# A state-space scan with hash routing: the spreading of states, the first routing steps and the first parity masks change engine and place

## The chip, the cores and the metric

The kernel runs on one core of a Trainium2 chip. A core has five engines, each with a queue of its own that it works off in order: TensorE (PE in the profile; PEld are its weight loads), VectorE (DVE), ScalarE (ACT), GpSimd (POOL) and SyncE (SP), which here only issues DMAs. They wait for one another through semaphores. The metric is the time of one execution on the device in microseconds; lower is better.

## The reference

A Mamba-2 scan (4 batches, 8 heads, 768 positions, head width 32, 16 states) writes a tensor of 3072 tokens by 256, and a mixture of 8 experts runs on it, each token going to the expert that a hash of its id names:

```python
log_a = np.log(np.clip(a, 1e-06, 1.0))
for c in range(nc):                       # chunks of 32 positions
    cum = np.cumsum(log_a[chunk])
    M = (Cc @ Bc.T) * np.exp(cum_i - cum_j) * causal
    y[chunk] = M @ xc + (Cc @ state) * np.exp(cum)
    state = np.exp(sum(log_a[chunk])) * state + (Bc * np.exp(cum_last - cum)).T @ xc
x = y.transpose(0, 2, 1, 3).reshape(3072, 256)
expert = token_ids * 2654435761 % 8
for e in range(8):
    out[expert == e] = np.maximum(x[expert == e] @ w1[e], 0) @ w2[e]
```

## The kernel before

The program has three parts: a prologue (decays, first batch's transposes), the scan over 24 output chunks of 128 positions (six a batch), and the expert layers, which gather the stored tokens by indirect DMA and scatter the results the same way. In the first two parts the order on each engine is the order in which the code is written.

The work is in steps of 64 positions, 12 to a batch. For a batch `b` the code names its steps so:

- `rows(b, i)`: scales B (i = 0) or C (i = 1) by decay factors; VectorE for batch 0, GpSimd for the others. `put_steps` and `get_steps` send the scaled B through memory (`b_steps`) and back as `bs`, in another layout; for batch 0 `turn_steps` does this on TensorE.
- `turn_b`, `turn_c`: eight transposes each on TensorE into PSUM (`tp`, two buffers), evicted by ScalarE to `bt`, `ct` and the two parity masks `ce` (C with the heads of one parity kept). `cp` is C times the step's decay, on GpSimd.
- `states(b, half)`: small products on TensorE (24 or 20), then on VectorE the recurrence `st` over six or five steps, each reading the product in PSUM.
- `blocks`: spreads each state over a block matrix `up`, with zeros for the other heads, by a product with a 0/1 pattern `own`.
- `grams(gc)`: the products of B and C for chunk `gc` (`gram`, two PSUM buffers), then on VectorE `m`, the causal mask times them.
- `outputs(gc)`: y in PSUM (`y_ps`, one buffer) from `cp` and `up` (line 487), and from x and `m` (line 496); ScalarE copies it to `y_sb`, SyncE stores it to `y_tokens`.

The loop over `gc` does `grams(gc + 1)`, `outputs(gc)`, the next piece of `routing()`, then, by the chunk's place in its batch, one of the steps of the next batch and a load. `routing()` is a generator that finds, from the token ids, where each token goes: `eid`, `mask`, counts by two matmuls (220, 221) into a `gram` buffer, a scan `pre`, the number of overflow tiles `nov`, `jump`, `val`, `slot`, `past`, four products `at`, three products `of`, 24 index matmuls (299) and `tokens`. Each `yield` ends a piece. The weights of the first three experts are loaded from ScalarE's queue from chunk 7 on.

`spin` issues matmuls whose result nobody reads; they are fillers on TensorE. In the prologue there are 10 on `ones`, 6 on `cum` and 2 more on `ones`.

## Time and profile before

| | us |
|---|---|
| median of 3 runs | 329.01 (327.29 to 330.5) |
| the profiled execution | 330.96, its span 329.2 |
| TensorE busy | 283.1 (86% of the span), 2507 matmul records |
| VectorE, GpSimd, ScalarE busy | 105.7, 102.9, 54.0 |
| mean granted TensorE clock | 0.885 |
| last y matmul of the scan | about 102.4 |
| first matmul of the expert layers | 117.30 |

The profile gives times from the start of the span. [...] Idle time of an engine is put down to what ended it (the releaser). A row of the timeline may merge neighbours of one kind: x20 is twenty of them, and a float32 matmul has two records. The expert layers run at the full clock with TensorE nearly always busy; the prologue and the scan, a third of the time, are where engines wait.

### The profile page before, as it was taken

Reading aid. Unit: us, or ns where it says so; the run is one execution under the profiler, and the core shown is the slowest. Engines: PE = TensorE matmul, PEld = TensorE weight load, DVE = VectorE, ACT = ScalarE, POOL = GpSimd, SP = SyncE. Lnnn points to the kernel's source line nnn. Section 1 sums busy time; section 2 is a strip of 40 time slices with the busy share of each in tenths; the row PEclk is TensorE's granted clock in tenths of the full one; section 3 lists DMA queues with packets and bytes.
Section 4 is the critical chain, followed back from the end, with each engine's and each line's share of the span. In section 5 each row is a group of like instructions: output and inputs, shape, how many; then the busy total and the mean of one; then the engine's idle time right before and its main releaser. Section 6 shows DMA issues by size and latency. Waiting matters only on the chain.

```text
span 329.2 us, 6084 instructions
## 1 busy us (share of the span) xinstructions
PE 283.1 (86%) x2507; PEld 178.5 (54%) x2507; DVE 105.7 (32%) x215; ACT 54.0 (16%) x116; POOL 102.9 (31%) x115
## 2 busy tenths in 40 slices
PE   7925986979983189999999999999999999999930
PEld 7724875858863045555555555555555555555510
DVE  3484489796541111211311211211211311211110
ACT  4300232415111001011111111111111111111110
POOL 6343045461210571311611612612611202202240
PEclk9997576585779559999999999999999999999985
DMA  7995379597479120144233243243342000000110
GB/s 124 157 132 147 77 142 195 143 223 196 137 244 324 52 81 28 32 148 142 73 144 138 82 151 126 84 156 114 90 169 96 31 2 16 31 0 19 34 48 2
DMA packets 56384, 35.65 MB, mean 108 GB/s; under 512 B 34911, under 2 KB 52345, under 8 KB 56356
## 3 DMA queue, kind: packets, MB, share of 16 engines
q1 hardware_dynamic: 49508, 22.41, 29.9%
q0 software_dynamic: 2816, 6.56, 6.3%
q10 hardware_dynamic: 4032, 6.29, 5.8%
q8 instruction: 20, 0.33, 0.4%
q14 instruction: 8, 0.07, 0.1%
HBM read 27.78 MB, written 7.73 MB: 108 GB/s over the span
## 4 chain that ended last, share of the span: by engine, by line
PE 53%; issue 19%; DVE 11%; DMA 10%; POOL 4%; ACT 1%; POOLq 0%; ACTq 0%; DVEq 0%
PE h_ps L613 18%; PE o_ps L622 16%; DMA out_dram<-o_sb,idx_out 6%; PE gram L470 4%; PE y_ps L496 4%; DVE st L449 3%; PE tp L404 3%; POOL out_dram L583 3%; PE y_ps L487 2%; DMA y_tokens<-y_sb 2%; PE y_ps L165 2%; PE tp L442 2%; PE xt_ps L601 1%; DVE m L474 1%; DVE at L286 1%
## 5 line engine op out<-in xcount | busy, mean ns | idle before, releaser
L613 PE MATMUL h_ps<-xT,w 128*128 128x416 f32 x256 | 102.7, 526 | 0.3 <-DVE xT L602 0.3
L622 PE MATMUL o_ps<-hT,w 128*128 128x416 f32 x256 | 102.1, 518 | 0.0
L622 PEld LDWEIGHTS o_ps<-hT,w 128*128 128x128 f32 x256 | 47.5, 190 | 40.1 <-issue 36.3
L583 POOL DMA_INDIRECT out_dram<-o_sb,idx_out x32 | 31.2, 976 | 114.0 <-ACT o_sb L642 95.8
L613 PEld LDWEIGHTS h_ps<-xT,w 128*128 128x128 f32 x256 | 47.5, 196 | 32.8 <-issue 31.1
L578 POOL DMA_INDIRECT xg<-y_tokens,idx_in x32 | 32.0, 1001 | 50.8 <-issue 20.1
L608 DVE TENSOR_SCALAR hT<-h_ps 128x416 f32<-128x416 f32 x32 | 18.9, 592 | 75.3 <-PE h_ps L613 75.3
L602 DVE COPY xT<-xt_ps 128x256 f32<-128x256 f32 (+1 forms) x32 | 12.0, 375 | 76.6 <-PE xt_ps L601 76.6
L606 ACT ACTIVATE hT<-h_ps 128x416 f32<-128x416 f32 x32 | 16.5, 517 | 99.8 <-PE h_ps L613 96.0
L496 PE MATMUL y_ps<-x_t,m 64*64 64x32 f32 x768 | 20.5, 250 | 7.3 <-DVE m L474 7.3
L496 PEld LDWEIGHTS y_ps<-x_t,m 64*64 64x64 f32 x768 | 20.0, 175 | 8.8 <-DVE m L474 8.7
L601 PE MATMUL xt_ps<-ident,xg 128*128 128x128 f32 (+1 forms) x64 | 12.6, 280 | 12.0 <-DMA xg<-y_tokens,idx_in 11.3
L474 DVE TENSOR_TENSOR m<-gram,causal 128x512 f32<-128x512 f32 x24 | 16.4, 687 | 17.9 <-PE gram L470 17.9
L601 PEld LDWEIGHTS xt_ps<-ident,xg 128*128 128x128 f32 (+1 forms) x64 | 8.4, 147 | 25.1 <-issue 23.0
L470 PE MATMUL gram<-ce,bt 32*64 32x128 f32 x384 | 21.1, 349 | 0.1
L457 POOL TENSOR_TENSOR up<-st,own 128x640 f32<-128x640 f32 (+1 forms) x8 | 13.1, 1640 | 24.2 <-DVE st L449 21.8
L500 ACT ACTIVATE y_sb<-y_ps 128x256 f32<-128x256 f32 x24 | 9.2, 383 | 63.1 <-PE y_ps L496 63.1
L642 ACT ACTIVATE o_sb<-ot_ps 128x256 f32<-128x256 f32 x16 | 6.1, 383 | 60.2 <-PE ot_ps L639 60.2
L470 PEld LDWEIGHTS gram<-ce,bt 32*64 32x64 f32 x384 | 13.6, 168 | 3.2 <-issue 2.1
L426 POOL TENSOR_TENSOR cp<-ct,step 128x768 f32<-128x768 f32 x4 | 6.1, 1529 | 26.1 <-ACT ct L417 26.1
L487 PE MATMUL y_ps<-up,cp 64*64 64x128 f32 x176 | 13.5, 359 | 0.6 <-ACT y_sb L500 0.6
L639 PE MATMUL ot_ps<-ident,oT 128*128 128x128 f32 (+1 forms) x64 | 12.2, 275 | 1.2 <-ACT oT L631 0.6
(123 smaller groups left out, 188.8 us busy)
## 6 DMA issues: line engine op xcount, KB each, us to landing
w<-in_moe_w_dram SPq DMA_DIRECT2D x20, 512.0 KB, 4.5
w<-in_moe_w_dram ACTq DMA_DIRECT2D x12, 512.0 KB, 5.4
y_tokens<-y_sb SPq DMA_DIRECT2D x24, 128.0 KB, 3.7
bc<-in_B_dram SPq DMA_DIRECT2D x4, 384.0 KB, 6.5
bc<-in_C_dram SPq DMA_DIRECT2D x4, 384.0 KB
x_t<-in_x_dram SPq DMA_DIRECT2D x4, 384.0 KB, 8.5
x_t<-in_x_dram SPq DMA_DIRECT2D x16, 96.0 KB, 3.3
b_steps<-rows SPq DMA_DIRECT2D x3, 384.0 KB, 4.0
```

The costliest lines, as they stand in the source:

```text
L457: eng.tensor_tensor(out=ups[b][:, k0:k1], in0=sts[b][:, k0:k1].unsqueeze(2).to_broadcast(sh), in1=own.rearrange("p g e d -> p g (e d)").un ...
L470: nc.tensor.matmul(out=gram[q * HL:(q + 1) * HL, g, u * P:(u + 1) * P], lhsT=bts[b][rr, 2 * c + u], rhs=ces[b][rr, :, 2 * c + u], start=Tr ...
L474: nc.vector.tensor_tensor(out=m.rearrange("p g u e i -> p g (u e i)"), in0=gram[:, :, 0:2 * P], in1=causal.rearrange("p (g x) i -> p g (x ...
L487: nc.tensor.matmul(out=y_ps[u * HL:(u + 1) * HL, q, 0:P], lhsT=cps[b][w, k], rhs=ups[b][w, k].rearrange("p g x -> p (g x)"), start=True, s ...
L496: nc.tensor.matmul(out=y_ps[u * HL:(u + 1) * HL, q, h * D:(h + 1) * D], lhsT=m[w, g, u, e], rhs=xs[b][w, h, k], start=(k == 0 and h == 0), ...
L578: nc.gpsimd.indirect_dma_start(out=dst, out_offset=None, in_=y_dram[:], in_offset=bass.IndirectOffsetOnAxis(ap=idx, axis=0), bounds_check= ...
L583: st = nc.gpsimd.indirect_dma_start(out=out[:], out_offset=bass.IndirectOffsetOnAxis(ap=idx, axis=0), in_=src, in_offset=None, bounds_chec ...
L601: nc.tensor.transpose(out=tp[:, i, 0:r], in_=g[0:r, i * P:(i + 1) * P], identity=ident[0:r, 0:r])
L606: nc.scalar.activation(o, i, AF.Relu)
L608: nc.vector.tensor_scalar_max(out=o, in0=i, scalar1=0.0)
L613: nc.tensor.matmul(out=hp, lhsT=w1s[e][:, i, f * P:(f + 1) * P], rhs=xT[e][:, i], start=(i == 0), stop=(i == DP - 1))
L622: nc.tensor.matmul(out=oP[e][:, j, 0:CAP], lhsT=w2s[e][:, f, j * P:(j + 1) * P], rhs=h, start=(f == 0), stop=(f == FP - 1))
```

## The change

- `blocks` no longer runs on GpSimd. The first piece of batch 0 stays on VectorE; every other call becomes four ScalarE instructions, one for each pair of pattern column and parity, with the 0/1 value as the scale. The calls stand later: one chunk behind the `states` whose result they spread.
- `routing()` is started at the top of the scan; its first piece stands before `turn_c(0)`, its second behind it, its third before the second `turn_steps`. So every later piece falls two chunks earlier than before.
- The second and third product `of` move from VectorE to GpSimd.
- The prologue has 3 fillers on `cum` instead of 6, and the 2 on `ones` are gone.
- The parity masks of batch 0 are four ScalarE instructions, two small ones (the first two steps) first; before, ScalarE did one parity and VectorE the other, in halves.

The diff:

```diff
--- before.py
+++ after.py
@@ -290,9 +290,9 @@
         nc.vector.tensor_tensor(out=of[:, 2], in0=iota_c.unsqueeze(1).to_broadcast(shc),
                                 in1=scol.unsqueeze(2).to_broadcast(shc), op=OP.is_equal)
         yield
-        nc.vector.tensor_tensor(out=of[:, 0], in0=of[:, 2], in1=iota_b.unsqueeze(2).to_broadcast(shc), op=OP.mult)
-        yield
-        nc.vector.tensor_tensor(out=of[:, 1], in0=of[:, 2], in1=one_ub.unsqueeze(2).to_broadcast(shc), op=OP.mult)
+        nc.gpsimd.tensor_tensor(out=of[:, 0], in0=of[:, 2], in1=iota_b.unsqueeze(2).to_broadcast(shc), op=OP.mult)
+        yield
+        nc.gpsimd.tensor_tensor(out=of[:, 1], in0=of[:, 2], in1=one_ub.unsqueeze(2).to_broadcast(shc), op=OP.mult)
         yield
         inv_ps = ps_t.tile([P, 512], F32, name="tp")[:, 0:2 * NM].rearrange("p (i x) -> p i x", i=2)
         for c in range(NCH):
@@ -318,7 +318,7 @@
     fac = apre.tile([NR, 2, BH, RS], F32)
     nc.scalar.activation(fac[:, 0], rel, AF.Exp, scale=-1.0)
     nc.scalar.activation(fac[:, 1], rel, AF.Exp)
-    spin(flat(cum), 6)
+    spin(flat(cum), 3)
 
     totx = apre.tile([NR, BH, NS], F32)
     step = const.tile([P, NB, NU], F32)
@@ -418,10 +418,9 @@
             if not first:
                 for e in range(2):
                     nc.scalar.activation(ce[:, e, :, rs], v, AF.Identity, scale=par[:, e:e + 1])
-        for p in range(0, NR, NR // 2) if first else ():
-            ps = slice(p, p + NR // 2)
-            nc.scalar.activation(ce[:, 0, ps], ct[:, ps], AF.Identity, scale=par[:, 0:1])
-            nc.vector.tensor_scalar(out=ce[:, 1, ps], in0=ct[:, ps], scalar1=par[:, 1:2], scalar2=None, op0=OP.mult)
+        for ps in (slice(0, 2 * RU), slice(2 * RU, NR)) if first else ():
+            for e in range(2):
+                nc.scalar.activation(ce[:, e, ps], ct[:, ps], AF.Identity, scale=par[:, e:e + 1])
         cp = abat.tile([P, NU, HL], F32, name="cp")
         nc.gpsimd.tensor_tensor(out=cp, in0=ct.rearrange("p (k c) r -> p k (c r)", c=RU),
                           in1=step[:, b].unsqueeze(2).to_broadcast([P, NU, HL]), op=OP.mult)
@@ -449,13 +448,19 @@
                 nc.vector.scalar_tensor_tensor(out=st[:, k + 1], in0=st[:, k], scalar=step[:, b, k:k + 1],
                                                in1=tp[:, i * PW:(i + 1) * PW], op0=OP.mult, op1=OP.add)
 
-    def blocks(b, k0, k1, eng):
+    def blocks(b, k0, k1, first=False):
 
         if b not in ups:
             ups[b] = abat.tile([P, NU, 2, PW], F32, name="up")
-        sh = [P, k1 - k0, 2, PW]
-        eng.tensor_tensor(out=ups[b][:, k0:k1], in0=sts[b][:, k0:k1].unsqueeze(2).to_broadcast(sh),
-                                in1=own.rearrange("p g e d -> p g (e d)").unsqueeze(1).to_broadcast(sh), op=OP.mult)
+        if first:
+            sh = [P, k1 - k0, 2, PW]
+            nc.vector.tensor_tensor(out=ups[b][:, k0:k1], in0=sts[b][:, k0:k1].unsqueeze(2).to_broadcast(sh),
+                                    in1=own.rearrange("p g e d -> p g (e d)").unsqueeze(1).to_broadcast(sh), op=OP.mult)
+            return
+        for g in range(2):
+            for e in range(2):
+                ds = slice(e * D, (e + 1) * D)
+                nc.scalar.activation(ups[b][:, k0:k1, g, ds], sts[b][:, k0:k1, ds], AF.Identity, scale=hm[:, g, e:e + 1])
 
     ms = {}
 
@@ -500,22 +505,23 @@
         nc.scalar.activation(y_sb, y_ps[:, :, 0:P], AF.Copy)
         nc.sync.dma_start(out=y_dram[gc * P:(gc + 1) * P, :], in_=y_sb.rearrange("p q d -> p (q d)"))
 
+    todo = iter(routing())
     rows(0, 0, nc.vector)
     turn_b(0)
     rows(0, 1, nc.vector)
     steps()
     heads()
-    spin(ones, 2)
+    next(todo)
     turn_c(0, True)
+    next(todo)
     turn_steps(0, 0)
     grams(0)
     states(0, 0)
-    blocks(0, 1, 2, nc.vector)
-    blocks(0, 2, UH + 1, nc.gpsimd)
+    blocks(0, 1, 2, True)
+    blocks(0, 2, UH + 1)
     rows(1, 0, nc.gpsimd)
-    todo = iter(routing())
+    next(todo)
     turn_steps(0, 1)
-    next(todo)
     for gc in range(NCH):
         b, c = divmod(gc, R)
         if gc + 1 < NCH:
@@ -523,12 +529,13 @@
         outputs(gc)
         if gc == 0:
             states(0, 1)
-            blocks(0, UH + 1, NU, nc.gpsimd)
         next(todo, None)
 
         b, c = divmod(gc - (b == 0), R)
         nb = max(b, 0) + 1
         after = nb + 1
+        if gc == 1:
+            blocks(0, UH + 1, NU)
         if gc == 0:
             put_steps(1)
             rows(1, 1, nc.gpsimd)
@@ -542,17 +549,18 @@
                 rows(after, 0, nc.gpsimd)
         elif c == 2 and nb < NB:
             states(nb, 0)
-            blocks(nb, 1, UH + 1, nc.gpsimd)
             if after < NB:
                 put_steps(after)
                 if after == 2:
                     load_bc(3)
         elif c == 3 and nb < NB:
+            blocks(nb, 1, UH + 1)
             states(nb, 1)
-            blocks(nb, UH + 1, NU, nc.gpsimd)
-        elif c == 4 and after < NB:
-            get_steps(after)
-            rows(after, 1, nc.gpsimd)
+        elif c == 4 and nb < NB:
+            blocks(nb, UH + 1, NU)
+            if after < NB:
+                get_steps(after)
+                rows(after, 1, nc.gpsimd)
         if after < NB and gc > 0 and c < 4:
             load_x(after, c)
         if gc > 6 and gc % 2 == 1 and gc < 23:
```

On TensorE and VectorE, in the prologue, the order now has the routing's first matmuls and its first VectorE instructions between the transposes of batch 0. TensorE before, from the fillers on `cum` to the second Gram product (`eid_r`: expert ids; `mask`: one-hot experts):

```order
L165 MATMUL y_ps<-cum,ident 128x256 x6
L404 MATMUL tp<-ident,rows 128x96 x8
L346 MATMUL tp<-step_w,totx 128x12 x4
L165 MATMUL y_ps<-ones,ident 128x128 x2
L404 MATMUL tp<-ident,rows 128x96 x8
L393 MATMUL tp<-ident,bt 64x64 x12
L470 MATMUL gram<-ce,bt 64x128 x8
L442 MATMUL tp<-x_t,bs 32x64 x24
L393 MATMUL tp<-ident,bt 64x64 x12
L209 MATMUL gram<-ident,eid_r 128x24
L470 MATMUL gram<-ce,bt 64x128 x8
```

and of the change, the same place:

```order
L165 MATMUL y_ps<-cum,ident 128x256 x3
L404 MATMUL tp<-ident,rows 128x96 x8
L346 MATMUL tp<-step_w,totx 128x12 x4
L209 MATMUL gram<-ident,eid_r 128x24
L404 MATMUL tp<-ident,rows 128x96 x8
L220 MATMUL gram<-mask,ones 128x192
L221 MATMUL gram<-mask,upto 128x192
L393 MATMUL tp<-ident,bt 64x64 x12
L475 MATMUL gram<-ce,bt 64x128 x8
L441 MATMUL tp<-x_t,bs 32x64 x24
L393 MATMUL tp<-ident,bt 64x64 x12
L475 MATMUL gram<-ce,bt 64x128 x8
```

The `eid_r` matmul stood between the state products and the second Gram product, the counting matmuls (220, 221) stood after the first y; all three now stand ahead of the state products.

VectorE in the scan, where the first states of batch 1 are made, in chunk 3; `slot_i` and its neighbours are the routing's slot arithmetic, `past` the piece behind it, and `m` the masked products for the next chunk. Before:

```order
L250 TENSOR_TENSOR jump<-tend,tiles 128x8
L251 SCALAR_TENSOR_TENSOR jump<-jump,past_185 128x8
L254 TENSOR_TENSOR val<-pre,cnt 128x192
L255 TENSOR_TENSOR val<-val,pre 128x192
L257 SCALAR_TENSOR_TENSOR cnt<-val,jump 128x192
L447 COPY st<-tp 128x64
L449 SCALAR_TENSOR_TENSOR st<-st,step,tp 128x64 x5
L474 TENSOR_TENSOR m<-gram,causal 128x512
```

and of the change:

```order
L265 TENSOR_REDUCE slot<-val 128x24
L268 CAST slot_i<-slot 128x24
L269 TENSOR_SCALAR slot_i<-slot_i 128x24
L271 CAST scol<-slot_i 128x24
L272 SCALAR_TENSOR_TENSOR srow<-scol,slot 128x24
L446 COPY st<-tp 128x64
L448 SCALAR_TENSOR_TENSOR st<-st,step,tp 128x64 x5
L479 TENSOR_TENSOR m<-gram,causal 128x512
```

Before, the piece with `jump` stood in front of the first `st` of batch 1; now the slot arithmetic, two pieces further, stands there.

GpSimd from batch 0's `cp` on, with - for before and + for the change:

```order
-L426 TENSOR_TENSOR cp<-ct,step 128x768
-L457 TENSOR_TENSOR up<-st,own 128x640
+L425 TENSOR_TENSOR cp<-ct,step 128x768
+L369 TENSOR_TENSOR rows<-bc,fac 96x8x8x16 x2
+L425 TENSOR_TENSOR cp<-ct,step 128x768
+L369 TENSOR_TENSOR rows<-bc,fac 96x8x8x16 x2
+L425 TENSOR_TENSOR cp<-ct,step 128x768
 L369 TENSOR_TENSOR rows<-bc,fac 96x8x8x16
-L457 TENSOR_TENSOR up<-st,own 128x640
+L293 TENSOR_TENSOR of<-of,iota_b 128x768
 L369 TENSOR_TENSOR rows<-bc,fac 96x8x8x16
```

The `up` instructions between the `rows` are gone, so a batch's `cp` and the next batch's two `rows` follow each other directly; the first `of` product stands between the last two `rows`. On SyncE one more thing moves: the load of `nov` into a register now stands behind the second y store, ahead of the read-back of batch 1's `bs`; before it stood among the last y stores.

## Rows read from the trace of the kernel before

**Rows 1.** Waits of TensorE, 0 to 117 us: us in total, times, longest.

```profile
PE y_ps L496 <- DVE m L474: 7.3, 5, 2.6
```

**Rows 2.** Timeline, 20 to 32 us: start, us, engine, line, operation, [idle].

```profile
20.71 1.53 POOL L457 TENSOR_TENSOR up<-st,own 128x640 f32<-128x640 f32 x1 [3.57 <-DVE st L449]
...
21.22 1.10 DVE L205 TENSOR_SCALAR eid_i<-tok 24x128 int32<-24x128 int32 x1
...
22.20 1.92 POOL L369 TENSOR_TENSOR rows<-bc,fac 96x1024 f32<-96x1024 f32 x1
...
22.35 1.85 DVE L207 CAST eid_r<-eid_i 24x128 f32<-24x128 int32 x1
...
24.26 0.24 PE L209 MATMUL gram<-ident,eid_r 24*128 24x24 f32 x1 [4.66 <-DVE eid_r L207]
...
29.86 1.70 DVE L216 TENSOR_TENSOR mask<-eid,iota_e 128x192 f32<-128x192 f32 x1
...
31.71 0.98 PE L220 MATMUL gram<-mask,ones 128*128 128x192 f32 x2 [3.59 <-DVE mask L216]
```

**Rows 3.** Groups by form: busy us, mean ns, idle before, releaser.

```profile
L254 DVE TENSOR_TENSOR val<-pre,cnt 128x192 f32<-128x192 f32 x1 | 0.3, 346 | 0.0
...
L474 DVE TENSOR_TENSOR m<-gram,causal 128x512 f32<-128x512 f32 x24 | 16.4, 687 | 17.9 <-PE gram L470 17.9
...
L449 DVE SCALAR_TENSOR_TENSOR st<-st,step,tp 128x64 f32<-128x64 f32 x40 | 11.2, 280 | 3.2 <-PE tp L442 1.9
...
L394 DVE COPY bs<-tp 128x384 f32<-128x384 f32 x2 | 1.1, 548 | 0.0
...
L349 ACT ACTIVATE step<-tp 128x48 f32<-128x48 f32 x1 | 0.2, 210 | 0.8 <-PE tp L346 0.8
...
L423 ACT ACTIVATE ce<-ct,par 128x384 f32<-128x384 f32 x2 | 1.1, 608 | 0.0
...
L500 ACT ACTIVATE y_sb<-y_ps 128x256 f32<-128x256 f32 x24 | 9.2, 383 | 63.1 <-PE y_ps L496 63.1
...
L457 POOL TENSOR_TENSOR up<-st,own 128x640 f32<-128x640 f32 (+1 forms) x8 | 13.1, 1640 | 24.2 <-DVE st L449 21.8
```

**Rows 4.** Stretches: PE, PEld, DVE, ACT, POOL busy; PEclk, DMA, GB/s.

```profile
32.00:45.00 13.00, 13.00 (x236) 10.88 (x235) 6.06 (x16) 4.88 (x11) 3.67 (x3) 0.50 0.47 83
45.00:51.00 6.00, 4.72 (x180) 3.61 (x172) 5.72 (x13) 0.77 (x2) 2.85 (x2) 1.00 0.75 186
```

**Rows 5.** Timeline, stations of TensorE and three rows of VectorE.

```profile
6.62 4.92 PE L165 MATMUL y_ps<-cum,ident 96*128 96x256 f32 x12
...
11.38 0.82 PE L404 MATMUL tp<-ident,rows 96*128 96x96 f32 x8
...
17.88 0.88 PE L442 MATMUL tp<-x_t,bs 64*32 64x64 f32 x48 [1.15 <-DVE bs L394]
...
35.06 0.55 DVE L224 COPY cnt<-gram 128x384 f32<-128x384 f32 x1
...
39.03 0.17 DVE L233 TENSOR_TENSOR n<-pre 128x8 f32<-128x8 f32 x1
...
39.72 1.54 PE L404 MATMUL tp<-ident,rows 96*128 96x96 f32 x8
...
53.84 1.08 PE L496 MATMUL y_ps<-x_t,m 64*64 64x32 f32 x32 [2.62 <-DVE m L474]
...
54.87 1.85 DVE L269 TENSOR_SCALAR slot_i<-slot_i 128x24 int32<-128x24 int32 x1
...
74.50 1.54 PE L404 MATMUL tp<-ident,rows 96*128 96x96 f32 x8
```

**Rows 6.** DMA issues, from 9.3 to 9.6 us, then to 110.

```profile
bc<-in_B_dram SPq DMA_DIRECT2D x1, 384.0 KB, 7.7
...
b_steps<-rows SPq DMA_DIRECT2D x3, 384.0 KB, 4.0
...
bs<-b_steps SPq DMA_DIRECT2D x6, 192.0 KB, 4.3
```

## Prediction

> **What bounds the kernel now.** I read the waits of TensorE first, then the rows around the longest of them, then the clock by stretches, and last the chain at the end of the scan.
>
> Three of TensorE's waits up to 117 us are touched by the change: 7.3 us, five times, on the masked products `m` [rows 1], and one of 4.66 us on `eid_r` and one of 3.59 us on `mask`, both from the routing [rows 2]. The rows of 20 to 32 us say why these are so long [rows 2]. At 20.71 GpSimd begins to spread states (`up`), and VectorE's 24-partition `eid_i`, begun at 21.22, takes 1.10 us and ends when `up` does. GpSimd's `rows` runs 1.92 us from 22.20, and the little `eid_r` takes 1.85 us and ends with it. `mask` beside the next `up` takes 1.70 us; a product of the same 192 columns, `val`, has 346 ns without company [rows 3]. So a VectorE instruction with two operands in SBUF, or a small copy, waits for the GpSimd instruction that is running, and TensorE waits for VectorE. With an operand in PSUM it escapes: the 24 `m` take 687 ns in the mean, many of them beside GpSimd [rows 3].
>
> [...]
>
> Behind the scan come the last store, the gathers and the expert layers; they are untouched, and I carry them over unchanged.
>
> **The change part by part.** I write y(n) for the output step of chunk n and compare four stations of TensorE: the transposes that begin `turn_c(1)` (39.72), y(6) (53.84), `turn_b(3)` (74.50) [rows 5], and the end of the scan.
>
> *A. Up to 39.72.* Six fillers on `cum` take 4.92 us, 0.82 each [rows 5]. Three fewer let the first transposes go at 9.2 instead of 11.38, where `rows(0,0)` on VectorE (done about 9.1) stops them: 2.2 earlier. Until the first state products at 17.88 the old chain then runs 6.5 us, of which 1.15 was a wait for `bs` behind VectorE's parity masks (now on ScalarE) and about 0.5 the two other fillers. The new `eid_r` and counting matmuls add about 1.1 (0.24, and half of 0.98 twice, since the rows of before have them at half clock). 9.2 + 6.5 - 1.65 + 1.1 gives 15.2, and with some slack 15.5. The routing's steps themselves run at 11 to 13 us, when GpSimd has nothing to do, so at their free price (`val`, 0.35); if a GpSimd instruction fell there, 1.9.
>
> From 15.5: products 0.88 [rows 5], then a copy and five `st` of 0.28 with the gaps between them, some 1.8, to 18.2. New order on VectorE: the first `up` (about 0.3), `cnt` 0.55 [rows 5], a scan of about the same, the second `bs` copy 0.55 [rows 3]. GpSimd now starts `rows(1,0)` as soon as B of batch 1 lands (issued between 9.3 and 9.6, 7.7 us to land: about 17.1 [rows 6]), and holds the little `up` until 19.05; `cnt` ends at 19.85, and only then may the next Gram product overwrite the PSUM buffer of the counts. `rows(1,1)` holds the scan until about 21.1, `bs` ends at 22.2, the second products at 23.1, `st` at 24.7, the eight small instructions from `n` on (0.17 each [rows 5]) at 26.1, `m` for y(2) at 26.8. `turn_c(1)` follows at 27.3 with the full clock, at 28.6 with half. That is 11.1 to 12.4 earlier. A second path must keep up: y(0) near 22, `b_steps` just behind it and 4.0 to land, SP's load of `nov` (in front of the read-back now; `nov` is ready at about 26), the two read-backs and 4.3 to land [rows 6] put `bs` of batch 1 at 31.7 to 32.4, and TensorE wants it one chunk after `turn_c(1)`, at 30 to 32.6. So the early end of the walk is cut by this path, and I take **-11.5**.
>
> *B. To y(6).* Here a term goes the wrong way. Without `up` between them GpSimd runs `cp(1)`, `rows(2,0)`, `rows(2,1)` back to back, about 1.5 + 1.9 + 1.9 us, from the `ct` evictions on; and the routing has moved up two chunks, so that its slot arithmetic (`slot_i`, 1.85 us beside one `rows` in before [rows 5]) now stands in front of `st` and `m` of chunk 5. It may be held by none or by two of the three: 0 to 3.6 us. So y(4) comes at 36 to 39.7, and y(6), two chunks of 2.8 us (full clock) or 3.5 (half) later, at 41.6 to 46.7, a lead of 12.2 to 7.1; I take 9.5, so **+2**, nearer the two rows of 22 us, where two small instructions were held one after the other.
>
> *ScalarE's four pieces.* A set of `up` was 1.64 us on GpSimd in the mean; now it is four instructions of 160 or 192 columns. No row has this size: not under 0.21 us each (48 columns), not over 0.61 (384 columns) [rows 3]. I take 0.35, 1.4 us a set, 11 us for 32 instructions. Their cover is ScalarE's 63.1 us of waiting for y [rows 3]; each set is issued one chunk after its `st`, so it doesn't hold the queue for VectorE. Without that cover the next y store, and the single y buffer with it, waits up to 1.4 us, six times in batches 1 to 3. [...]
>
> *C. To `turn_b(3)`, 20.7 us in before* [rows 5]. The routing's long products (`at`, `of`) are held by `up` here as `mask` was; with `up` gone, one of them still falls behind `cp` and `rows`. Of the 7.3 us that TensorE waited for `m`, 2.62 belong to B, so up to 4.7 are here, just in front of it and in D; I take less than half, **-1.5** (0 to -4).
>
> *D. To the end of the scan.* The two `of` products move to GpSimd (about 1.6 each by `up`) and are due two chunks later: nothing, unless `rows(3,1)` between them delays the index matmuls, up to 2. The rest of those waits for `m`, behind the last batch's `up`, goes: **-1** (+2 to -3).
>
> Sum: -11.5 + 2 - 1.5 - 1 = **-12 us**. The profiled execution took 330.96 us (span 329.2), 1.95 over the median of 329.01; its difference put on the median gives **317.0**.
>
> **The rivals.**
> 1. *The clock stays up.* [...] From 39.72 on some 31 us are at half clock (the end of the stretch to 45 and two more of 13 us each); at the full clock's pace (180 matmul records in 4.72 us against 236 in 13.00 [rows 4]) up to 16 us would go, but VectorE is then nearly full, so I count half, 8 more: -20, **309**. Against it: every full-clock stretch of before ended in a wait for VectorE, and the state steps are still there.
> 2. *GpSimd's back-to-back block eats the gain.* The slot arithmetic is held twice, `m` of chunk 5 comes 4 us late, the clock falls once more: B costs 7 instead of 2, C and D bring nothing: -4.5 to -5, **324**. For it: the two consecutive holds at 21 and 22 us. [...]
> [...]
>
> **How the numbers follow.** The forecast 0.54 (alone 313 to 321, from B's and C's ends), rival 1 0.16, rival 2 0.22, rival 3 0.08. The range 309 to 325 leaves out part of 1, the upper end of 2, and 3. A per cent (3.3 us) is about what a measurement of this kernel can tell from no change. Faster by more: the forecast, rival 1 and half of rival 2, 0.82; within it: the rest of rival 2 and a mild case of 3, 0.12; slower 0.06.
>
> **What would show it.** A right: first state products near 15.5 us, no wait for `eid_r` or `mask`, `turn_c(1)` at 27 to 29. B: `slot_i` or the cast behind it over 1.5 us, y(4) waiting for `m`. ScalarE: `up` pieces of 0.3 to 0.4 us. The clock column tells rival 1 from the forecast: little 0.5 after 30 us. What would make the prediction wrong: the prologue's lead given back by late `bs` or `m` in batch 1, or the last stores and the weight loads, moved together, ending no earlier.

## The result, and the profile after

| | before | after | after, run again |
|---|---|---|---|
| median, us | 328.19 (4 times), 326.91 (11 times, beside the repeat) | 318.09 (314.8 to 320.0, 4 times) | 319.72 (317.6 to 322.2, 6 times) |
| ratio to before, 95% interval | | 0.9648 (0.955 to 0.975) | 0.9801 (0.975 to 0.985) |
| profiled execution, us | 330.96 | 314.81 | 317.61 |
| mean granted clock of it | 0.885 | 0.921 | 0.894 |
| TensorE, VectorE, ScalarE, GpSimd busy | 283.1, 105.7, 54.0, 102.9 | 267.7, 91.8, 65.3, 91.5 | |

The change makes the kernel faster, as forecast (317.0, range 309 to 325). How much is less sure than the first comparison says: its repeat gives 2 per cent, and over both sets the medians are 319.3 (ten times) against 327.4 (fifteen), 8 us. The ratios leave out executions more than 1.5 per cent above the fastest of their kernel, so they are not quite the quotients of the medians. The two profiles of the changed kernel differ; both are read here.

Waits of TensorE from 0 to 107 us in the first profile of after (us in total, times, longest; `...` stands for lines left out, here and below):

```profile
PE tp L441 <- DMA bs<-b_steps: 7.5, 4, 2.5
PE y_ps L501 <- issue: 4.5, 5, 1.2
...
PE y_ps L492 <- DVE up L457: 0.9, 1, 0.9
...
PE gram L475 <- issue: 0.7, 1, 0.7
PE y_ps L492 <- issue: 0.6, 1, 0.6
...
PE y_ps L501 <- DVE m L479: 0.5, 1, 0.5
```

The 7.3 us on `m` [rows 1] have become 0.5, and `eid_r` and `mask` (4.66 and 3.59 us [rows 2]) don't appear at all (in the repeat `eid_r` has 0.7 us, `m` and `mask` nothing). In their place stand two waits that before had not: 7.5 us for `bs` of batches 1 and 2, and 5.8 us for which the profile names no releaser (`issue`).

The timeline of the same execution, at the stations of the prediction:

```profile
11.09 0.21 DVE L205 TENSOR_SCALAR eid_i<-tok 24x128 int32<-24x128 int32 x1
11.33 0.22 DVE L207 CAST eid_r<-eid_i 24x128 f32<-24x128 int32 x1
...
12.22 0.36 DVE L216 TENSOR_TENSOR mask<-eid,iota_e 128x192 f32<-128x192 f32 x1
...
17.16 1.21 PE L441 MATMUL tp<-x_t,bs 64*32 64x64 f32 x48
...
28.16 0.88 PE L404 MATMUL tp<-ident,rows 96*128 96x96 f32 x8
...
32.26 1.85 DVE L269 TENSOR_SCALAR slot_i<-slot_i 128x24 int32<-128x24 int32 x1
32.98 0.30 PE L441 MATMUL tp<-x_t,bs 64*32 64x64 f32 x4 [2.52 <-DMA bs<-b_steps]
...
41.46 0.67 PE L501 MATMUL y_ps<-x_t,m 64*64 64x32 f32 x32 [0.49 <-DVE m L479]
...
51.53 1.56 PE L441 MATMUL tp<-x_t,bs 64*32 64x64 f32 x44 [2.27 <-DMA bs<-b_steps]
...
62.48 0.53 PE L404 MATMUL tp<-ident,rows 96*128 96x96 f32 x4
```

Beside GpSimd that had nothing to do, `eid_i`, `eid_r` and `mask` take 0.21, 0.22 and 0.36 us (1.10, 1.85 and 1.70 in [rows 2]). The times at which TensorE begins each station, with the lead over before [rows 5]; "repeat" is the second profile of after:

| TensorE begins | before | after | lead | repeat | lead |
|---|---|---|---|---|---|
| first state products | 17.88 | 17.16 | 0.7 | 16.16 | 1.7 |
| `turn_c(1)` | 39.72 | 28.16 | 11.6 | 29.28 | 10.4 |
| y(6), the products with `m` | 53.84 | 41.46 | 12.4 | 42.92 | 10.9 |
| `turn_b(3)` | 74.50 | 62.48 | 12.0 | 64.80 | 9.7 |
| last y | 101.98 | 86.69 | 15.3 | 92.85 | 9.1 |

The stretches of the first profile (busy us of PE, PEld, DVE, ACT, POOL, then PEclk, DMA, GB/s):

```profile
11.10:17.90 6.80, 6.76 (x84) 5.72 (x87) 2.04 (x7) 3.32 (x7) 2.88 (x2) 0.50 1.38 179
18.00:31.00 13.00, 9.76 (x328) 7.91 (x316) 10.80 (x38) 6.73 (x19) 2.59 (x3) 1.00 0.97 163
35.00:38.40 3.40, 3.40 (x96) 2.90 (x92) 3.19 (x9) 0.81 (x3) 0.97 (x1) 0.50 1.05 235
55.50:87.00 31.50, 26.27 (x916) 21.48 (x912) 14.73 (x36) 14.26 (x38) 6.26 (x4) 0.99 0.91 237
```

and one of the repeat:

```profile
22.50:40.00 17.50, 15.85 (x356) 13.34 (x360) 14.18 (x38) 6.50 (x17) 5.25 (x3) 0.53 0.98 194
```

and the first of these stretches in before:

```profile
11.10:17.90 6.80, 4.94 (x74) 4.12 (x72) 2.72 (x5) 3.08 (x7) 1.70 (x1) 1.00 1.38 178
```

PEclk is the granted clock of TensorE as a share of its full speed. In the prologue it is 0.50 where before it was 1.00, and from 55.5 us to the end of the scan it is 0.99. The repeat has the lower level for most of the time from 22.5 to 40 us (mean 0.53) and from 50 to 60 (0.55), and again in part of the last 20 (0.76 from 75 to 95). So the clock's phases are not fixed by the kernel, and the first profile has the favourable ones.

What the scale of 0 or 1 on ScalarE costs, by form (busy us, mean ns of one, idle before):

```profile
L463 ACT ACTIVATE up<-st,hm 128x160 f32<-128x160 f32 x20 | 6.9, 416 | 4.8 <-DVE st L448 4.8
...
L463 ACT ACTIVATE up<-st,hm 128x192 f32<-128x192 f32 x12 | 4.5, 443 | 0.2 <-DVE st L448 0.2
```

Neighbours overlap: a set of four takes 1.38 us (160 columns) or 1.48 (192), 11.4 us in all. The 11 us of the prediction hold. ScalarE still waits 33.6 us for y.

### The profile page after: what moved, and what is told of

It is laid out like the page before. It is cut to its first block, busy times and chain, and to the rows that moved or that the text cites. A ratio compares the mean times of both kernels' runs of the same rounds, so it can differ in the third digit from the quotient of the medians.

```text
span 313.1 us, 6085 instructions
## 1 busy us (share of the span) xinstructions
PE 267.7 (85%) x2497; PEld 165.5 (53%) x2497; DVE 91.8 (29%) x211; ACT 65.3 (21%) x150; POOL 91.5 (29%) x109
## 3 DMA queue, kind: packets, MB, share of 16 engines
q10 hardware_dynamic: 4032, 6.29, 6.9%
## 4 chain that ended last, share of the span: by engine, by line
PE 52%; issue 21%; DMA 12%; DVE 6%; POOL 5%; ACT 1%; POOLq 0%; SPq 0%; ACTq 0%; DVEq 0%
PE h_ps L621 18%; PE o_ps L630 17%; DMA out_dram<-o_sb,idx_out 6%; PE gram L475 3%; PE y_ps L501 3%; POOL out_dram L591 3%; PE y_ps L492 2%; DMA bs<-b_steps 2%; PE tp L441 2%; DVE st L448 2%; PE xt_ps L609 1%; DMA y_tokens<-y_sb 1%; PE tp L404 1%; DMA a_t<-in_a_dram 1%; PE ot_ps L647 1%
## 5 line engine op out<-in xcount | busy, mean ns | idle before, releaser
L621 PEld LDWEIGHTS h_ps<-xT,w 128*128 128x128 f32 x256 | 47.2, 195 | 32.4 <-issue 30.8
L501 PE MATMUL y_ps<-x_t,m 64*64 64x32 f32 x768 | 18.2, 226 | 4.9 <-issue 4.5
L609 PE MATMUL xt_ps<-ident,xg 128*128 128x128 f32 (+1 forms) x64 | 12.6, 280 | 11.4 <-DMA xg<-y_tokens,idx_in 10.6
L479 DVE TENSOR_TENSOR m<-gram,causal 128x512 f32<-128x512 f32 x24 | 16.4, 687 | 14.1 <-PE gram L475 14.1
L501 PEld LDWEIGHTS y_ps<-x_t,m 64*64 64x64 f32 x768 | 17.1, 145 | 4.7 <-issue 3.7
L475 PE MATMUL gram<-ce,bt 32*64 32x128 f32 x384 | 17.7, 298 | 0.7 <-issue 0.7
L505 ACT ACTIVATE y_sb<-y_ps 128x256 f32<-128x256 f32 x24 | 9.3, 389 | 34.8 <-PE y_ps L501 33.6
L441 PE MATMUL tp<-x_t,bs 64*32 64x64 f32 x352 | 9.4, 248 | 7.7 <-DMA bs<-b_steps 7.5
L492 PE MATMUL y_ps<-up,cp 64*64 64x128 f32 x176 | 11.8, 315 | 2.1 <-DVE up L457 0.9
L441 PEld LDWEIGHTS tp<-x_t,bs 64*32 64x32 f32 x352 | 7.4, 126 | 10.4 <-DMA bs<-b_steps 3.6
```

The lines of the kernel that those rows point to most:

```text
L441: nc.tensor.matmul(out=tp[32 * r:32 * r + 32, i * PW:(i + 1) * PW], lhsT=bs[w, k, 32 * g:32 * g + 32], rhs=xb[w, 2 * g:2 * g + 2, k], star ...
L475: nc.tensor.matmul(out=gram[q * HL:(q + 1) * HL, g, u * P:(u + 1) * P], lhsT=bts[b][rr, 2 * c + u], rhs=ces[b][rr, :, 2 * c + u], start=Tr ...
L479: nc.vector.tensor_tensor(out=m.rearrange("p g u e i -> p g (u e i)"), in0=gram[:, :, 0:2 * P], in1=causal.rearrange("p (g x) i -> p g (x ...
L492: nc.tensor.matmul(out=y_ps[u * HL:(u + 1) * HL, q, 0:P], lhsT=cps[b][w, k], rhs=ups[b][w, k].rearrange("p g x -> p (g x)"), start=True, s ...
L501: nc.tensor.matmul(out=y_ps[u * HL:(u + 1) * HL, q, h * D:(h + 1) * D], lhsT=m[w, g, u, e], rhs=xs[b][w, h, k], start=(k == 0 and h == 0), ...
L609: nc.tensor.transpose(out=tp[:, i, 0:r], in_=g[0:r, i * P:(i + 1) * P], identity=ident[0:r, 0:r])
```

## Experiments

Ratios are to the kernel before, run beside each on the same chip. Those of after are 0.965 and 0.980; what lies between is not told from it.

### The routing back at its old place

```diff
-    todo = iter(routing())
     rows(0, 0, nc.vector)
...
-    next(todo)
     turn_c(0, True)
-    next(todo)
...
     rows(1, 0, nc.gpsimd)
-    next(todo)
+    todo = iter(routing())
     turn_steps(0, 1)
+    next(todo)
```

> The changed kernel with one part undone: the routing is started where it stood before (its first piece behind the second `turn_steps`, the others in the loop). Two theories of where the 10 us come from. Theory 1, the place of the routing: its first steps now run while GpSimd has nothing to do and TensorE would wait anyway. Then this kernel gives most of term A back: `turn_c(1)` 6 to 9 us later than the 28.16 of the changed kernel, the time 6 to 9 us above it (324 to 327). Theory 2, the engine of `up`: GpSimd no longer holds VectorE, so `eid_i`, `eid_r` and `mask` are short at their old place too (0.2 to 0.4 us, against 1.10, 1.85 and 1.70 in [rows 2]); then `turn_c(1)` comes at most 3 us later and the time stays within 0 to 3 us (318 to 321).

Measured: 324.68 us, ratio 0.992 (0.988 to 0.997). `turn_c(1)` begins at 35.46, 7.3 us later than after. Its timeline:

```profile
20.67 1.93 POOL L369 TENSOR_TENSOR rows<-bc,fac 96x1024 f32<-96x1024 f32 x1 [0.35 <-DMA bc<-in_C_dram]
20.86 1.81 DVE L205 TENSOR_SCALAR eid_i<-tok 24x128 int32<-24x128 int32 x1
...
22.98 0.30 PE L209 MATMUL gram<-ident,eid_r 24*128 24x24 f32 x1 [3.40 <-DVE eid_r L207]
...
29.23 0.98 PE L220 MATMUL gram<-mask,ones 128*128 128x192 f32 x2 [2.25 <-DVE mask L216]
```

Without `up` on GpSimd it is `rows` that holds `eid_i`, for 1.81 us. `eid_r` (0.21 us) and `mask` (0.36) are short, as theory 2 said, and TensorE waits 3.40 and 2.25 us for them all the same. The hold of `eid_i` is worth 1.6 of these 5.6 us (1.81 less its free 0.21); for the rest they stand behind other work on VectorE at the old place. Theory 1 holds: without the early place 6.6 us of the first comparison's 10.1 are gone, or 5.4 by the median of all ten times of after. Whether that is more than half of the gain depends on which comparison of after one takes (0.965 or 0.980, against 0.992).

### The early routing alone, in the kernel before

The same lines of the routing, the other way round, in the kernel before.

> The kernel before with one part of the change alone: the routing starts at the top of the scan (first piece ahead of `turn_c(0)`, second behind it, third ahead of the second `turn_steps`), all fillers stay, `up` and `of` stay where they were. Undoing the routing's place in the changed kernel cost about 6.6 us, undoing the engine of `up` 2.3. Theory 1 (the two are separate terms): 6 to 7 us faster than before, 321 to 322, `turn_c(1)` near 30 to 32. Theory 2 (they need each other: with `up` still on GpSimd the early lead is lost to `m`, `at` and `of` held by it): at most 3 us faster, 325 and up, with 5 us and more of waits for `m`.

Measured: 324.47 us, ratio 0.990 (0.985 to 0.995), 3.2 us and not 6 to 7; `turn_c(1)` at 32.78. Its timeline and a row of its waits:

```profile
15.77 0.97 PE L220 MATMUL gram<-mask,ones 128*128 128x192 f32 x2 [3.19 <-DVE mask L216]
```

```profile
PE y_ps L496 <- DVE m L474: 4.7, 3, 3.0
```

The time lies between the ranges of the two theories. `mask` itself takes 0.36 us here, but it stands behind the parity masks, which this kernel keeps on VectorE: 3.2 us that neither theory had in mind. TensorE also waits for `m`, once for 3.0 us, about as theory 2 said. Whether the parts need each other stays open: 0.990 for the place alone and 0.992 for everything else multiply to 0.982, which is the repeat of after (0.980; separate terms), but not its first comparison (0.965).

### `up` back on GpSimd

```diff
-        for g in range(2):
-            for e in range(2):
-                ds = slice(e * D, (e + 1) * D)
-                nc.scalar.activation(ups[b][:, k0:k1, g, ds], ..., scale=hm[:, g, e:e + 1])
+        nc.gpsimd.tensor_tensor(out=ups[b][:, k0:k1], ..., op=OP.mult)
```

> The changed kernel with one part undone: `up` goes back to GpSimd, as one instruction a set, at the new places (one chunk behind the states). Theory 1 (place of the routing): the prologue keeps its lead, `turn_c(1)` within 1.5 us of 28.16; later some `m`, `at` and `of` are held by `up` again, 2 to 4 us in all: 320 to 322. Theory 2 (engine of `up`): most of the gain is lost, 7 to 10 us: 325 to 328, with waits of TensorE for `m` of 5 us and more again (0.5 in the changed kernel).

Measured: 320.40 us, ratio 0.981 (0.971 to 0.991). The holds are back, in the timeline

```profile
44.35 1.92 DVE L286 TENSOR_TENSOR at<-iota_p,srow 128x768 bf16<-128x768 f32 x1
...
44.49 0.67 PE L500 MATMUL y_ps<-x_t,m 64*64 64x32 f32 x32 [1.56 <-DVE m L478]
```

(`at` takes 0.95 in after), but TensorE waits for `m` only this once. `turn_c(1)` comes at 31.27, not within 1.5 us of 28.16 as theory 1 said; but with the code of after up to that point it came anywhere from 28.16 to 31.33 (in the profiles of after, `w1_after` and `of_vector`). The time is theory 1's and can't be told from after's. Theory 2 falls: all four times (319.8 to 322.9) are below all ten of the kernel with the late routing (323.1 to 327.0), so the place is worth more than the engine of `up`. Whether the engine of `up` is worth anything at these places stays open between 0 and 1.6 per cent.

### The fillers back, twice

```diff
-    spin(flat(cum), 3)
+    spin(flat(cum), 6)
...
+    spin(ones, 2)
```

> The changed kernel with the five fillers back (6 on `cum`, 2 on `ones`). In the changed kernel the granted clock is 0.5 from 11.09 to 17.92 us; before it was 1.0 up to 24.5. Theory 1: the fillers kept that clock, but cost what they gave: the first transposes begin near 11.4 instead of 9.15 (2.2 later), the work up to the first state products runs at the full clock and takes 2 to 2.5 us less; first state products at 17 to 17.5 (17.16 in the changed kernel) and the time within 1.5 us of it. Rival: fewer fillers carry a part of term A by themselves, as the prediction had it: the first state products 2 us later, at 19, and the time 2 us longer (320).

> The changed kernel with all the old fillers once more, for a closer interval: its first one (0.9535 to 0.9796, median 316.5) doesn't tell it from the changed kernel. Theory 1: the clock that the fillers keep in the prologue (first state products at 15.05 us against 17.16) is worth 1 to 2 us at the end, ratio 0.003 to 0.006 below that of the changed kernel. Rival: the lead is lost to the lower clock from 22 to 45 us that followed in its profile, and the two are within 1 us.

Measured: ratios 0.967 (0.954 to 0.980) and 0.978 (0.972 to 0.983), medians 316.54 and 319.53. In the first profile the clock stays up in the prologue (0.9 or more in the page's slices up to 15.6 us), its timeline has

```profile
13.47 0.92 PE L393 MATMUL tp<-ident,bt 64*64 64x64 f32 x24
...
15.05 0.87 PE L441 MATMUL tp<-x_t,bs 64*32 64x64 f32 x48
...
17.80 1.20 DVE L457 TENSOR_TENSOR up<-st,own 128x128 f32<-128x128 f32 x1
```

so the first states come 2.1 us earlier than in after, which neither expectation of the first run had (17 to 17.5, or 19). Nearly half of that is lost at once, as `rows(1,0)` now holds the little `up`. In the second profile they come at 16.59, and the 24 transposes ahead of them (L393) take 1.55 us. Run beside each other, this kernel and after are 0.2 us apart: the rival of the second run holds, and that taking fillers away was a part of the gain can't be seen. With six fillers on `cum` the first transposes begin at 8.92 and 9.08 us here, with three at 9.15 and 8.78 in after.

### `bs` sent and read back earlier

```diff
     rows(1, 0, nc.gpsimd)
+    put_steps(1)
+    get_steps(1)
...
         elif c == 3 and nb < NB:
             blocks(nb, 1, UH + 1)
             states(nb, 1)
+            if after < NB:
+                get_steps(after)
```

(and taken out at the old places)

> The changed kernel with the way of `bs` through memory begun earlier: for batch 1 the write of `b_steps` and the read-back are issued directly behind `rows(1,0)` instead of behind the stores of chunks 0 and 1, for the later batches the read-back is issued one chunk earlier. In the changed kernel the state products of batches 1 and 2 wait for `bs` four times, 7.5 us in all. Theory 1: these waits are on the path, so they go and the time falls by 4 to 7 us (311 to 314), and the output steps from y(4) on come 2 to 4 us earlier, from y(9) on 4 to 7. Rival: the waits stand in front of work that VectorE or the lower clock would hold anyway; then they go too, but `m`, `st` or a longer stretch of clock 0.5 takes their place and the time falls by less than 2 us (316 to 318).

Measured: 319.83 us, ratio 0.978 (0.968 to 0.988): not faster than after. Its waits, 0 to 107 us:

```profile
PE y_ps L501 <- issue: 6.6, 4, 3.0
PE y_ps L492 <- DVE up L457: 2.4, 1, 2.4
PE y_ps L501 <- DVE m L479: 2.2, 2, 1.1
PE tp L441 <- DMA x_t<-in_x_dram: 1.4, 1, 1.4
```

None is for `bs` any more, and 12.6 us are for other things. Theory 1 falls. The time is that of after or more, above the rival's range too (316 to 318), but its mechanism is there: the two waits for `m` are at y(5) and y(6), behind the slot arithmetic that after's wait for `bs` had covered. The 2.4 us on `up` come from its hold by `rows(1,0)`; the next kernel has 2.5 with `bs` unmoved, so they are not a result of this edit.

### `of` back on VectorE, and the masks split as before

```diff
-        nc.gpsimd.tensor_tensor(out=of[:, 0], ...
+        nc.vector.tensor_tensor(out=of[:, 0], ...
```

(and `of[:, 1]` alike)

> The changed kernel with one part undone: the second and third `of` products go back to VectorE. In the changed kernel they take 1.47 and 1.46 us on GpSimd. VectorE is busy 91.8 us of 313 there and TensorE waited only 0.5 us for `m`. Theory 1 (VectorE has the time): within 1 us of the changed kernel (317 to 319). Rival: each of them, 0.95 us or more on VectorE and held by `rows` or `cp`, stands in front of an `m`: 1 to 3 us longer, with waits for `m` in chunks 8 to 12.

Measured: 320.19 us, ratio 0.975 (0.968 to 0.982). `of` takes 0.95 us on VectorE at 62.29 and 63.76, no `m` is late there. The move changes nothing that can be measured, which is theory 1's mechanism; the median lies 1 us above its range. TensorE waits for `m` earlier on, at y(5) and y(6), in the timeline

```profile
42.12 0.67 PE L501 MATMUL y_ps<-x_t,m 64*64 64x32 f32 x32 [0.92 <-DVE m L479]
...
44.98 0.67 PE L501 MATMUL y_ps<-x_t,m 64*64 64x32 f32 x32 [1.15 <-DVE m L479]
```

In this execution `bs` of batch 1 was not late; the `of` products come 17 us after.

```diff
-                nc.scalar.activation(ce[:, e, ps], ct[:, ps], AF.Identity, scale=par[:, e:e + 1])
+            nc.scalar.activation(ce[:, 0, ps], ...)
+            nc.vector.tensor_scalar(out=ce[:, 1, ps], ...)
```

> The changed kernel with one part undone: the parity masks of batch 0 as before, one parity on ScalarE and one on VectorE, in halves. The prediction gave the masks' move a part of term A: the `bs` copy no longer stands behind them on VectorE (1.15 us in [rows 5]). Theory 1: the first state products come 0.5 to 1.2 us later and the time is up to 1 us longer. Rival: since the counting products now stand between, VectorE has the time, and four masks on ScalarE (2.13 us) are the longer way: 0 to 1 us shorter.

Measured: 319.19 us, ratio 0.976 (0.969 to 0.982), no difference from after. The profiled execution, the longest of its four (322.61), shows what theory 1 had in mind, and more, in its timeline:

```profile
17.35 1.98 DVE L216 TENSOR_TENSOR mask<-eid,iota_e 128x192 f32<-128x192 f32 x1
...
19.38 1.01 PE L220 MATMUL gram<-mask,ones 128*128 128x192 f32 x2 [4.75 <-DVE mask L216]
```

`mask`, behind the VectorE masks, falls beside `rows(1,0)` and takes 1.98 us. First state products come at 23.26, so theory 1's 0.5 to 1.2 us is far too little for this execution. The other three times are 317.5 to 320.2; whether those executions escape the hold is not shown.

### The weights out of the scan

```diff
-        if gc > 6 and gc % 2 == 1 and gc < 23:
-            i = (gc - 7) // 2
-            load_w(i // 4, nc.scalar, [i % 4])
...
+    load_w(0, nc.scalar)
+    load_w(1, nc.scalar)
     for k in range(KT):
         turn_x(0, k)
```

> The changed kernel without any expert weights loaded during the scan: the loads of experts 0 and 1 (eight transfers of 512 KB, issued from chunk 7 to 21) stand behind the scan instead. This is a probe, not a version: the first expert must wait for its weights. It is for the waits that the profile puts down to `issue`, 5.8 us in the scan of the changed kernel and none of them in the scan of before; each long one ends 1.2 to 1.5 us after a 16 KB packet of the instruction queue (packet 77.39 to 78.32, wait until 79.79). Theory 1 (TensorE runs out of instructions because their packets come late among the bulk transfers): from 50 us on, where the weights were loaded, these waits fall from 3.9 us to under 1, and the scan ends 2 to 4 us earlier; those before 30 us stay. Theory 2 (the packets are asked for too late whatever the traffic is): the waits stay at 3 to 5 us. The whole time is 5 to 15 us longer in both.

What ran was another treatment than the text says: behind the scan the order is the scheduler's, and it issued these loads in the prologue, as the queue of ScalarE shows. All weights came between 0 and 40 us. There is still none in the second half of the scan, so those waits can be compared. Measured: 323.57 us, ratio 0.986 (0.983 to 0.990). DMA queues from 20 to 40 us (packets, MB, share of 16 engines), then a row of the timeline and the same row of after, then the waits from 50 to 103 us:

```profile
q1 hardware_dynamic: 9775, 1.83, 73.0%
q10 hardware_dynamic: 2347, 3.09, 51.9%
```

```profile
37.45 0.19 PE L501 MATMUL y_ps<-x_t,m 64*64 64x32 f32 x1 [2.03 <-issue]
```

```profile
22.74 0.19 PE L501 MATMUL y_ps<-x_t,m 64*64 64x32 f32 x1 [1.21 <-issue]
```

```profile
PE gram L475 <- issue: 0.4, 1, 0.4
PE y_ps L501 <- issue: 0.3, 1, 0.3
```

Where the weights (q10) no longer are, the waits put down to `issue` are 0.7 us instead of 3.9, as theory 1 said. The clock does not explain it away: from 80 to 100 us, where both short waits are, the granted clock is 1.00 and TensorE busy 18.6 of 20 us, with a DMA share of 0.28; in after the share is 0.90 from 60 to 87. But it is one execution. The wait at 37.45 says nothing on the weights, although they are loading there: after has it at the same matmul, the last of y(0), with no weights loading. The scan ends no earlier, against theory 1, since the weights now share the DMA engines with the prologue's loads: from 20 to 40 us B takes 14.1 us to land (6.9 in after), the first state products come at 30.09, the last y at 101.78.

> The changed kernel with the loads of the second expert's weights (2 MB) moved from chunks 15 to 21 of the scan to the first step of the expert layers, and those of the third from its second step to its third. If the late instruction packets come from the weights' traffic (theory 1 of the run without weights in the scan), the waits at 74.62, 79.79 and 83.79 (2.5 us) go and the time falls by 1 to 3 us. If the traffic doesn't matter, or if the loads collide with the gathers at 94 to 101 us instead, it stays within 1 us or grows.

Here too the scheduler took the moved loads (the second expert's and the third's) ahead, into 40 to 85 us, and the traffic there became denser (from 40 to 85 us the weights' queue has 6.29 MB and 46.0 per cent of the engines, 4.93 MB and 38.4 in after). Measured: 322.41 us, ratio 0.986 (0.979 to 0.993), 6.5 us of waits put down to `issue`. It says nothing on later loads; loads that are really later weren't tried.

### The changed kernel again, and all repairs together

> The changed kernel itself, unaltered, beside the next three, since its first comparison (ratio 0.9648, interval 0.955 to 0.975) rests on four times between 314.8 and 320.0, and its profiled execution (314.81, clock 0.921) is the shortest of them. Theory 1: the gain of some 3.5 per cent holds, ratio 0.960 to 0.972. Theory 2: the first set was a lucky one, since most kernels with one part undone came out at 0.975 to 0.98; then the ratio is 0.972 to 0.98. What varies from one execution to the next should be where the clock falls to 0.5 and how long the first `up` on VectorE is held by `rows(1,0)` on GpSimd (0.29 us in the profiled execution, 1.2 to 1.9 in three of the kernels with one part undone).

Measured: 319.72 us, ratio 0.980 (0.975 to 0.985), theory 2. Two waits of its profile, 0 to 107 us:

```profile
PE tp L441 <- DMA bs<-b_steps: 6.4, 4, 2.8
PE y_ps L501 <- issue: 6.1, 3, 3.3
```

The last kernel has the old fillers, the earlier `bs`, and

```diff
-    blocks(0, 1, 2, True)
+    blocks(0, 1, 2)
```

> The changed kernel with three additions: the old fillers, `bs` of the later batches sent and read back earlier (as in the run before), and the first piece of `up` on ScalarE too, so that no VectorE instruction of batch 0's first output waits for `rows(1,0)` on GpSimd. In the profiles so far the first output waited 0.9 to 2.5 us for that `up`; four small ScalarE instructions should take some 0.9 us. Theory 1 (each removes a wait on the path): first y products near 18.5 us (20.69 in the changed kernel), no wait for `bs` in batches 1 and 2, 312 to 315 us. Rival: the freed time goes to a lower clock or to waits for instructions, as in the run with earlier `bs` alone: 316 to 319, with more than 5 us of waits put down to `issue` or of additional clock 0.5.

Measured: 317.77 us (315.0 to 319.1), ratio 0.972 (0.966 to 0.977). Its median is 2.0 us below that of after beside it, but the intervals overlap a little: it is the best of its set, and not shown to beat after. Its timeline:

```profile
17.91 0.33 PE L492 MATMUL y_ps<-up,cp 64*64 64x128 f32 x2
...
18.12 0.51 PE L501 MATMUL y_ps<-x_t,m 64*64 64x32 f32 x16
21.11 0.63 PE L501 MATMUL y_ps<-x_t,m 64*64 64x32 f32 x11 [2.48 <-issue]
```

The first y begins 2.8 us earlier than in the first profile of after (20.69) without any wait for `up`, and 16 products later TensorE waits 2.48 us, put down to `issue`. Of that lead 1.2 us are left at the next state products (21.68 against 22.86). The waits went as theory 1 said (none for `bs`, none for `up`), and the time is the rival's, with 7.1 us of waits put down to `issue`.

## Why the prediction was right, and where it was wrong

**A, -11.5 to `turn_c(1)`: right in size, 11.6 and 10.4, in part by luck.** The routing's first steps run at their free price, as said. But the first 2.2 us of the sum, from three fillers less, are not the change's. The six fillers of [rows 5] take 4.92 us in this one execution of before; in the four profiles of variants that have six they take 2.84, 2.84, 2.86 and 3.33, and the first transposes begin at 8.81 to 9.48 us, as with three. And the station itself varies: four profiles with the code of after up to there have 28.16, 29.28, 29.91 and 31.33, leads of 11.6 to 8.4. Of the other steps two were off. The first state products were to come at 15.5 and came at 17.16 and 16.16, since the granted clock was 0.50 from 11.10 to 17.90 us, and 0.56 from 13 to 16 in the repeat; the half clock of rival 3 did occur, but it ended with the prologue. The hold of the little `up` by `rows(1,0)` is real but not in every execution (0.29, its free price, and 0.46 us in the two profiles of after, 1.2 to 1.9 in three variants).

**B, +2 to y(6): wrong in sign.** The lead was to shrink to 9.5 and is 12.4 and 10.9. Rival 2's collision took place in full: three slot instructions in a row (1.01, 1.85 and 1.85 us from 31.21 on), one more than the two that I allowed. It cost at most the 0.5 us for which y(6) waits, since TensorE was waiting for `bs` then, 2.5 and 0.8 us. I put that path at 31.7 to 32.4 and cut A for it; it ended at 33 to 34, behind the station and under the same wait. Two delays lay beside each other, and I had added them. Two profiles of variants show it: where `bs` of batch 1 is not late, the same hold is followed by waits for `m` at y(5) and y(6) of 2.2 us (`bs` earlier) and 2.1 (`of` on VectorE), and that is the +2 of the term. I had also counted only one of the two waits for `m` that before has between the stations; besides the 2.62 us [rows 5] there is

```profile
49.49 0.67 PE L496 MATMUL y_ps<-x_t,m 64*64 64x32 f32 x32 [1.26 <-DVE m L474]
```

So 3.9 us of waiting went in this stretch and 3.8 came (3.3 for `bs`, 0.5 for `m`): the lead hardly moves, and C and D had 3.4 us of waits for `m` to win, not 4.7.

**C, -1.5, and D, -1: the sizes failed.** The leads go 12.4, 12.0, 15.3 in the first profile and 10.9, 9.7, 9.1 in the repeat. The waits for `m` went, as the terms say. What these steps didn't ask is what is late next: `bs` of batch 2, 4.3 us (4.8 in the repeat), whose read-back stood behind a y store, and the waits put down to `issue`, 3.9 and 5.1 us from 60 on. Where the clock stays up all through D (0.99 from 55.5 to 87 us), 3.3 us are won nevertheless; where it doesn't (0.76 from 75 to 95), 0.6 is lost.

**The edits costed at nothing were right:** `of` on GpSimd (1.47 and 1.46 us each, 1.6 said), ScalarE's `up` (1.38 and 1.48 us a set, 1.4 said). A single piece is shown with 416 or 443 ns in the mean, neighbours overlapping, above the 0.3 to 0.4 us that were to be the sign.

**The sum, -12 against a measured -10.1 and -7.2.** The forecast time of 317.0 lies 1.1 us below the first median and 2.7 below the second. Beside the two new waits one thing made the sum too large: the profile of before was of an execution of 330.96 us, longer than any of the fifteen times beside it (323.9 to 330.5). The gain between profiled executions is 16.2 and 13.4 us. So the rows that I priced hold more time than a median execution does, the fillers above among it, and I put the whole difference on the median. That this explains the rest is an inference; no median execution of before was profiled.

**The rivals.** The first one, the clock that stays up, is the first profile from 55 us on, and that execution of 314.81 us is the shortest of ten; it is a matter of the execution, not of the kernel. The second's mechanism was there, without its price where `bs` covered it. The third, half clock throughout, had 6.8 us of it in the prologue of the first profile and 3 in the repeat's. Its chance also supposed that the fillers had kept the clock up in before, which no run shows: with all of them, the 24 transposes of the prologue take 0.92 us in two profiles of variants (`fillers`, `combined`) and 1.55 in two (`fillers_again`, `before_early`), as in the repeat at 0.56. (The chances of the forecast, rival 1 and half of rival 2 add to 0.81, not 0.82.)

## What to carry to other kernels

Move small work that others wait for to a place where nothing stands in front of it, neither a long GpSimd instruction (`eid_r` took 1.85 us beside `rows`, 0.22 without company) nor a queue of other work; here this was worth more than the choice of engine for the long work. When a wait goes, ask for each later stage which other delay had been hidden behind it: two delays that overlap must not be added, and here waits for `bs` (7.5 us) and waits put down to `issue` (5.8) took the place of those for `m`, `eid_r` and `mask`. Price a change from a profile of a median execution, and measure a gain of a few per cent twice.

## What the runs showed of the hardware

**Some waits of TensorE end behind a packet of instructions.** Waits put down to `issue` of 0.4 us or more: none in the scan of before, 7 in after, 44 in all 13 profiles of after and the variants. Each of the 44 ends 1.3 to 1.8 us after a 16 KB packet of the instruction queue (q8) has ended; the packets are mostly 4 to 7 us apart, so this is no accident. That TensorE stands without instructions in these waits is inferred from it. One of the longest, in the first run with fillers: the packet begins at 82.51, when TensorE has been waiting for 1.1 us, and ends at 83.44.

```profile
84.74 0.87 PE L501 MATMUL y_ps<-x_t,m 64*64 64x32 f32 x24 [3.31 <-issue]
```

Its DMA queues from 82.4 to 83.5 us:

```profile
q10 hardware_dynamic: 295, 0.30, 77.6%
q1 hardware_dynamic: 101, 0.10, 25.2%
q8 instruction: 1, 0.02, 5.3%
```

The packet comes while the weights (q10) fill the engines. The row of this queue on the page of before, then on that of after:

```profile
q8 instruction: 20, 0.33, 0.4%
```

```profile
q8 instruction: 20, 0.33, 0.5%
```

So there are no more packets of instructions than before. My estimate is that TensorE gets to the end of them sooner: 41 of the 44 waits follow 5 us at a mean granted clock of 0.77 or more (the others 0.50, 0.53 and 0.69). In before a packet of 81.0 to 83.0 us, 2 us long, cost it nothing. That bulk transfers make these waits longer agrees with the run without weights in the second half (0.7 us instead of 3.9), but is not shown: the packets themselves took no less time there from 80 us on (1.1 to 1.5 us, against 0.9 to 1.5 in after from 55 us on), and the ten waits before 30 us come with no weights loading. What sets the time of a packet, no run here shows.

**The clock's phases differ between executions of one kernel.** In the two profiles of after the lower level (0.50) holds from 11.1 to 17.9 us and twice more up to 55 us, or from 22.5 to 40 us (mean 0.53) and later again, at 314.81 and 317.61 us. What makes the clock fall, no run here shows. Waits that come and go by a microsecond or two differ as well. The times of one set spread by 5 us, and in four to six of them a gain of 1 per cent can't be seen.
